# The q projection of two chunks as a Strassen pair, in a transformer layer with sliding attention and a gated FFN on one Trainium2 core

## The chip, the core and the metric

The kernel runs on one core of a Trainium2 chip. The core has a matrix engine (TensorE, PE in the profile), a vector engine (VectorE, DVE), a scalar engine (ScalarE, ACT), GpSimd (POOL) and SyncE (SP). SyncE, ScalarE and GpSimd also issue transfers, each in the order of its own instructions. The metric is the device time of one execution in microseconds. The kernel before was run 8 times: median 770.64 us, from 770.35 to 774.97.

## What is computed

The input x has 2048 rows of 1024 in bf16. First comes attention with 32 heads of 32: each position looks at 8 earlier ones, 2 apart. Then comes a feed-forward network with a product of two projections (F = 3584). Both are added to the input of their part. Cut to what matters:

```python
qkv = layernorm(x) @ wqkv                     # 1024 -> 3 x 1024
logits = sum_d(q[s] * k[s - 2 * w]) * Dh ** -0.5   # w = 0..7, masked where s - 2w < 0
o = sum_w(softmax(logits)[w] * v[s - 2 * w])
h = x + o @ wo
n = layernorm(h)
h2 = h + ((n @ w_gate) * (n @ w_up)) @ w_down
```

## The kernel before, in words

The rows are cut into four chunks of 512 (`TC`). A chunk's normalized rows are kept transposed in `lnT` (feature on the partition). A matmul multiplies a 128x128 block of weights with 128x512 of `lnT`; eight of them make one group for 128 output columns and 512 rows (`mm_group`, L429 to L432, the matmul is on L431). The constant `GROUP_US = 1.73` stands for its time. Its result lies in one of eight banks of psum.

*Projections.* `qkv(c, blocks)` (L434) goes through blocks of 512 columns; q is blocks 0 and 1, k 2 and 3, v 4 and 5. `evac_qkv` (L342) copies each result on ScalarE into a staging tile and stores it on SyncE's queue to `qd`, `kd` or `vd` in memory. `load_qk` and `load_v` (L448, L455) load it back on GpSimd's queue in another layout, with chunk part and head on the partitions, for attention.

*Attention.* `attention(c)` (L468 to L546) is a generator of VectorE work: eight products of q with shifted k (L477), folds over the 32 features (L479 to L487), softmax (Exp on ScalarE), eight products with v (L523) and their sums (L529 to L534). At its end the result `oD` is stored (L536) and loaded back transposed as `oT` in four parts (L539), all on GpSimd's queue, in that order. A chunk's attention starts when the one before has ended (L469).

*Output projection and norm.* `wo_ln2(0)` (L589 to L623) multiplies `oT` by `wo` (L602, 64 matmuls), adds the input on VectorE, and normalizes on VectorE: BATCH_NORM_STATS2 (L183), mean and variance, the row itself, then a transposed load on SyncE's queue. Chunks 1 and 2 use `wo_norm` (L569, matmul L578) and the generator `Norm2.finish` (L562), whose sums and rows are ScalarE's.

*FFN.* `ffn1_first` (L694) computes gate and up of chunk 0 in groups of eight matmuls in 7 blocks of 4; ScalarE copies each result, VectorE multiplies the two (L700). At (b, j) = (4, 2) it calls `wo_1`, which finishes attention 1, runs output projection 1 and starts its norm. `ffn1_second` does chunk 1. For chunks 2 and 3 the FFN already uses Strassen's scheme in Winograd's form (`weight_sums` L796, `activation_sums` L814, `product` L824, `pair_block` L829): of two chunks and two halves of the inner dimension, seven products in place of eight, in fp16 with a power of two as scale. Chunks 0 and 1's down product does the same (`ex`, `ev`, `ey`, `ez`, L944): its sums of weights (`t`, L937) are VectorE's. Class `Scale` (L628 to L656) finds such a power of two: sums of absolute values, one matmul that adds them over the partitions (`total`), a few VectorE operations on one column.

*Order.* No scheduler rearranges anything: each engine runs its instructions in the order in which the program emits them. The order is spread by `Background` (L37 to L75): after each group the main line calls `step(GROUP_US)`, which adds `rate` times that time to a credit, and the generators on its list are advanced until their own estimated times (what they `yield`) have used up the credit. VectorE work of the main line is taken off the credit by `spend`. `finish` runs a generator to its end. So VectorE's order is a mix of attention steps and of the main line's additions, products and norms, fixed when the program is built, and an instruction of VectorE that waits holds all that follows on it.

The main line (L875 to L916) is: q, k of chunk 0 with `load_qk(0)`; chunk 1's q and k; v of chunks 0 and 1; all of chunk 2; q and k of chunk 3; attention 0 is finished; `wo_ln2(0)`; v of chunk 3; the FFN of chunks 0 and 1 with `wo_1` inside; then `wo_adds(2)` (output projection 2, L998), the down products of chunks 0 and 1, `wo_adds(3)`, and the FFN of chunks 2 and 3.

Of the kernel before, what the change touches and what calls it, by code (L numbers as in the profile page):

```python
# [78 lines left out]
def kernel(  # L79
# [46 lines left out]


# [72 lines left out]
    def load_x(c, what, eng):  # L200
        tiles = []
        for t in range(4):
            xt = hp.tile([128, D], BF, tag="h", name=f"{what}{c}_{t}")
            eng.dma_start(xt[:], x[bass.ds(c * TC + t * 128, 128), :])
            tiles.append(xt)
        return tiles
# [52 lines left out]
    class NormOnScalar(Norm1):  # L259
# [16 lines left out]
        def devs(self):  # L276
            nc.scalar.activation(self.nm, self.s, ACTF.Copy, scale=-1.0 / D)
            for t in range(4):
                nc.scalar.activation(self.junk[:], self.xs[t][:], ACTF.Square, bias=self.nm[:, t:t + 1],
                                     accum_out=self.ss[:, t:t + 1])  # L280
                yield "later", self.pace
            nc.scalar.activation(self.rs4[:], self.ss, ACTF.Ln, bias=eps[:], scale=1.0 / D)
# [17 lines left out]
        def rows(self):  # L300
            for t in range(4):
                self.row(t)
                self.transpose(t)
                yield "later", self.pace

# [33 lines left out]

    qkv_in = {}  # L340

    def evac_qkv(c, m, ps):  # L342
        sg = t1k.tile([128, HB + TC], BF, tag="t1k", name=f"sg{c}_{m}")
        nc.scalar.copy(sg[:, HB:HB + TC], ps[:])  # L344
# [5 lines left out]
        if m < 8:  # L350
            nc.sync.dma_start(qd[c][:, 4 * hg:4 * hg + 4, :, :].rearrange("c g d s -> (g d) c s"),
                              sg[:, HB:HB + TC].rearrange("p (c s) -> p c s", c=4))
# [81 lines left out]
    def qkv(c, blocks, last=False):  # L434
        for b in blocks:
            for j in range(4):
                ps = psum.tile([128, TC], F32, tag="mm", name=f"ps{c}_{b}_{j}")
                mm_group(ps, wts["qkv", b], j, lnTs[c])
# [9 lines left out]
    def load_qk(c):  # L448
        qD = att.tile([128, DH, SUB], BF, tag="qD", name=f"qD{c}")
        kD = att.tile([128, DH, SUB + HB], BF, tag="kD", name=f"kD{c}")  # L450
        nc.gpsimd.dma_start(qD[:], qd[c].rearrange("c g d s -> (c g) d s"))
# [16 lines left out]
    def attention(c):  # L468
        while c and c - 1 not in over:  # L469
            yield "later", 1.0  # L470
# [79 lines left out]
    class Norm2(NormOnScalar):  # L550
# [11 lines left out]
        def finish(self):  # L562
            yield from self.devs()
            yield from self.rows()
# [4 lines left out]
    def wo_norm(c):  # L569
# [4 lines left out]
        for t in range(4):  # L574
            for hf in range(2):
# [6 lines left out]
                if hf == 0 and t > 0:  # L582
                    n.sum(t - 1)
                bg.step(GROUP_US)
        n.sum(3)
        retire(2)
        return n

    def wo_ln2(c, at={}):  # L589
        lnT = lnTp.tile([128, KO, TC], BF, tag="lnT", name=f"lnT2_{c}")  # L590
        hs = hss[c]
        mv4, rs4 = ln_tiles(f"2_{c}")

        def norm(t):
            ln = normalize(hs[t], mv4, rs4, t)
            nc.sync.dma_start_transpose(lnT[:, :, bass.ts(t, 128)], ln[:])

        for t in range(4):
            for hf in range(2):
                ps = psum.tile([128, 512], F32, tag="mm", name=f"wo{c}_{hf}_{t}")  # L600
                for kk in range(KO):
                    nc.tensor.matmul(ps[:], lhsT=oTs[c][:, kk, t, :], rhs=wts["wo", c, hf][:, kk, :],  # L602
                                     start=(kk == 0), stop=(kk == KO - 1))
                nc.vector.tensor_tensor(hs[t][:, bass.ts(hf, 512)], ps[:], hs[t][:, bass.ts(hf, 512)], ALU.add)
                if hf == 1:
                    stats(hs[t], mv4, t)
                    rstd_of(mv4, rs4, t, t + 1)
                    bg.spend(1.5)
                elif t > 0:
                    norm(t - 1)  # L610
                    bg.spend(0.55)
                bg.spend(0.7)
                if 2 * t + hf in at:
                    at[2 * t + hf]()
                bg.step(GROUP_US)
        norm(3)
        retire(2)
        for t in range(4):
            rows = hsd[c][:, t, :]
# [734 lines left out]
```

## Time and profile before

| | |
|---|---|
| median of 8 runs | 770.64 us |
| the profiled execution | 770.8 us |
| its span in the trace | 769.0 us |
| TensorE (PE) busy | 763.9 us, 99% |
| weight loads (PEld), beside PE | 350.9 us, 46% |
| VectorE (DVE) busy | 606.2 us, 79% |
| ScalarE (ACT) busy | 513.0 us, 67% |
| GpSimd (POOL) busy | 142.0 us, 18% |
| qkv projections on TensorE after 27.37 us | 136.52 us, 632 matmuls, then 13.81 us, 64 matmuls |
| output projection 0 | 163.89 us, 13.81 us long |
| FFN of chunk 0 starts | 191.51 us |
| output projection 1 starts | 253.67 us |

How to read it: in the page's second part each engine has 40 digits, one for each fortieth of the span (19.2 us), in tenths of busy time; PEclk is TensorE's granted clock in tenths. The chain of waits and the timelines begin a row with the start in us and the length in us, then engine, line and operation, and what is written from what, with a count at the end; a bracket has the idle time of the engine just ahead and what ended it. A row of the groups has a count, then the busy time in us and the mean in ns of one. Back-to-back operations of one engine overlap a little, so that a row's mean can be longer than the step from one to the next.

### The profile page before, as it was taken

What the parts mean: (1) busy time and instruction counts of PE and PEld (TensorE: products, weight loads), DVE (VectorE), ACT (ScalarE), POOL (GpSimd) and SP (SyncE); (2) the same over time, 40 slices, a digit from 0 to 9 for tenths busy, and PEclk for the clock granted to TensorE, in tenths of its full rate; (3) what the DMA queues carried; (4) which work ended last, traced back from release to release, by engine and by line L of the source; (5) the groups of instructions that cost most, each with busy time, mean ns of one, the idle gap of its engine ahead of it and who ended that gap; (6) DMA issues with size and microseconds to landing.
All of it is one profiled execution on the core that took longest, in us unless ns stands there. A gap on an engine that the chain in (4) does not pass through costs nothing.

```text
span 769.0 us, 10302 instructions
## 1 busy us (share of the span) xinstructions
PE 763.9 (99%) x3663; PEld 350.9 (46%) x3663; DVE 606.2 (79%) x718; ACT 513.0 (67%) x979; POOL 142.0 (18%) x152
## 2 busy tenths in 40 slices
PE   8999999999999999999999999999999999999998
PEld 6444444444444444444444444444444444444444
DVE  5629999999999999999998997985454444568863
ACT  4648966423677398777899986836777677788240
POOL 0000000200002000020000001018778677600000
PEclk9999999999999999999999999999999999999999
DMA  8999796999966689579559448673342423730001
GB/s 272 264 258 262 212 268 148 265 312 289 302 221 209 217 297 293 176 243 326 197 184 301 136 159 281 124 198 105 82 110 55 110 74 91 255 128 29 0 29 55
DMA packets 190915, 144.85 MB, mean 188 GB/s; under 512 B 81808, under 2 KB 181136, under 8 KB 188688
## 3 DMA queue, kind: packets, MB, share of 16 engines
q1 hardware_dynamic: 180416, 116.94, 53.9%
q0 software_dynamic: 3584, 22.02, 8.4%
q10 hardware_dynamic: 6864, 5.24, 2.4%
q8 instruction: 28, 0.46, 0.2%
q14 instruction: 23, 0.19, 0.1%
HBM read 110.10 MB, written 27.26 MB: 179 GB/s over the span
## 4 chain that ended last, share of the span: by engine, by line
PE 97%; DVE 2%; DMA 1%; issue 0%; ACTq 0%; DVEq 0%
PE ps L431 21%; PE dx L944 6%; PE py L826 6%; PE pwu L431 6%; PE pwg L431 6%; PE pg L431 6%; PE pz L826 6%; PE px L826 6%; PE pu L431 6%; PE wo L998 4%; PE pv L826 3%; PE ez L944 3%; PE ey L944 3%; PE ex L944 3%; PE dy L944 3%; PE wo L602 2%
## 5 line engine op out<-in xcount | busy, mean ns | idle before, releaser
L431 PE MATMUL ps<-lnT,w_qkv 128*128 128x512 bf16 x736 | 159.6, 379 | 0.0
L431 PEld LDWEIGHTS <-w_qkv 128*128 128x128 bf16 x736 | 71.8, 98 | 86.3 <-issue 0.4
L344 ACT CAST sg<-ps 128x512 bf16<-128x512 f32 x96 | 55.1, 586 | 47.1 <-PE ps L431 44.8
L477 DVE TENSOR_TENSOR prod<-qD,kD 128x4096 bf16<-128x4096 bf16 x32 | 72.2, 2286 | 12.6 <-DMA kD<-kd 12.6
L523 DVE TENSOR_TENSOR pv<-vD,at 128x4096 bf16<-128x4096 bf16 x32 | 72.4, 2286 | 0.2
L826 PEld LDWEIGHTS <-sw 128*128 128x128 f16 x448 | 43.8, 98 | 52.9 <-issue 0.2
L431 PEld LDWEIGHTS <-w_wg 128*128 128x128 bf16 x448 | 43.8, 98 | 52.9
L431 PEld LDWEIGHTS <-w_wu 128*128 128x128 bf16 x448 | 43.8, 98 | 52.9
L826 PE MATMUL px<-lnT,ws 128*128 128x512 bf16 x224 | 55.2, 379 | 0.0
L536 POOL DMA_DIRECT2D od<-oD x4 | 2.2, 544 | 275.8 <-DVE oD L534 275.8
L431 PE MATMUL pwu<-lnT,w_wu 128*128 128x512 bf16 x224 | 52.9, 379 | 0.0
L431 PE MATMUL pwg<-lnT,w_wg 128*128 128x512 bf16 x224 | 52.9, 379 | 0.0
L431 PE MATMUL pg<-lnT,w_wg 128*128 128x512 bf16 x224 | 52.9, 379 | 0.0
L431 PE MATMUL pu<-lnT,w_wu 128*128 128x512 bf16 x224 | 52.9, 379 | 0.0
L826 PEld LDWEIGHTS <-ws 128*128 128x128 f16 x336 | 32.9, 98 | 39.6
L807 POOL TENSOR_TENSOR sw<-ws 128x512 f16<-128x512 f16 x26 | 30.0, 1153 | 82.6 <-PE pv L826 49.1
L944 PEld LDWEIGHTS <-gs 128*128 128x128 f16 (+1 forms) x280 | 27.4, 98 | 33.1
L479 DVE TENSOR_TENSOR prod<-prod 128x4096 bf16<-128x4096 bf16 x16 | 36.6, 2290 | 0.4
L843 ACT COPY py<-px 128x512 f32<-128x512 f32 x28 | 16.0, 570 | 28.5 <-PE px L826 28.5
L808 POOL TENSOR_TENSOR sw<-sw,ws 128x512 f16<-128x512 f16 x26 | 30.0, 1155 | 2.0
L809 POOL TENSOR_TENSOR sw<-ws 128x512 f16<-128x512 f16 x26 | 30.0, 1155 | 0.0
L810 POOL TENSOR_TENSOR sw<-ws,sw 128x512 f16<-128x512 f16 x26 | 30.0, 1155 | 0.0
(334 smaller groups left out, 1474.7 us busy)
## 6 DMA issues: line engine op xcount, KB each, us to landing
w_wg<-in_B_w_gate_dram SPq DMA_DIRECT2D x14, 1024.0 KB, 7.2
w_wu<-in_B_w_up_dram SPq DMA_DIRECT2D x14, 1024.0 KB, 6.6
w_pair<-in_B_w_gate_dram SPq DMA_DIRECT2D x14, 512.0 KB, 4.0
w_pair<-in_B_w_up_dram SPq DMA_DIRECT2D x14, 512.0 KB, 5.3
w_wo<-in_A_wo_dram SPq DMA_DIRECT2D x6, 1024.0 KB, 7.7
w_qkv<-in_A_wqkv_dram SPq DMA_DIRECT2D x5, 1024.0 KB, 11.6
kd<-sg SPq DMA_DIRECT2D x32, 144.0 KB, 4.4
kD<-kd POOLq DMA_DIRECT2D x4, 1152.0 KB, 9.0
```

Of the source, the lines that this page charges most:

```text
L344: nc.scalar.copy(sg[:, HB:HB + TC], ps[:])
L431: nc.tensor.matmul(ps[:], lhsT=wt[:, ko, bass.ts(j, 128)], rhs=rhs[:, ko, :], start=(ko == 0), stop=(ko == KO - 1))
L477: nc.vector.tensor_tensor(prod[:, j], qD[:], kD[:, :, o:o + SUB], ALU.mult)
L479: nc.vector.tensor_tensor(prod[:, :, 0:16], prod[:, :, 0:16], prod[:, :, 16:32], ALU.add)
L523: nc.vector.tensor_tensor(pv[:, j], vD[:, :, o:o + SUB], at[:, w, None, :].to_broadcast((128, DH, SUB)), ALU.mult)
L807: eng.tensor_tensor(sw[:, i, 0], a21, a22, ALU.add)
L808: eng.tensor_tensor(sw[:, i, 1], sw[:, i, 0], a11, ALU.subtract)
L809: eng.tensor_tensor(sw[:, i, 2], a11, a21, ALU.subtract)
L810: eng.tensor_tensor(sw[:, i, 3], a12, sw[:, i, 1], ALU.subtract)
L826: nc.tensor.matmul(ps[:], lhsT=lhs[:, ko, :], rhs=rhs[:, ko, :], start=(fresh and ko == 0), stop=(ko == 3), skip_group_check=not fresh)
L944: nc.tensor.matmul(ps[:, bass.ds(lo, n)], lhsT=lhs[k][:, bass.ts(q, 128)], rhs=rhs[k][:, bass.ds(lo, n)], start=(fresh and k == 0), stop=( ...
L998: nc.tensor.matmul(ps[:], lhsT=oTs[c][:, kk, t, :], rhs=wts["wo", 2, hf][:, kk, :], start=(kk == 0), stop=(kk == KO - 1))
```

## The change

The q projection (blocks 0 and 1) of chunks 2 and 3 is computed together by the same seven-product scheme. The two row halves are the two chunks, the two inner halves are the halves of the 1024 features, and the two output halves are blocks 0 and 1. For each of four positions m the program makes seven products of four matmuls. `q_pair(0)` does two of the four before output projection 0, `q_pair(2)` the others behind it, with two groups of chunk 3's v in between.

What this needs: a power of two as scale for q's weights (four sums of absolute values, two on VectorE, two on ScalarE, and one small matmul); the conversion of both weight blocks to fp16 in place (VectorE); 16 sums of weights (VectorE); sums of the two chunks' `lnT` (`q_row_sums`, 12 operations, and `q_last_sum`, one, VectorE). Of the 16 results eight are evacuated by ScalarE and eight by VectorE, which adds the product `p5` from a staging tile. Chunk 1's q uses the converted weights too.

Around it: the order of the projections is other; attention 1 does not start before `q_last_sum`; the load of chunk 3's x waits for the landing of chunk 0's k, and the load of chunk 0's q for the transposes of chunk 1 (one-element copies on GpSimd that touch both). Output projection 0 uses `wo_norm` with `devs=False`: sums and squares on ScalarE, the four rows on VectorE in place of BATCH_NORM_STATS2; the rate of `Background` is 1.06 after it (1.03 before). The steps of `abs_down` are closer together, and a scale's total in `wo_adds(2)` comes two groups later. The diff, cut to its core:

```diff
-    def load_x(c, what, eng):
+    def load_x(c, what, eng, after=None):
         tiles = []
         for t in range(4):
             xt = hp.tile([128, D], BF, tag="h", name=f"{what}{c}_{t}")
+            if after is not None and t == 0:
+                nc.gpsimd.tensor_copy(xt[:, 0:1], after)
...
+        def row_on_vector(self, t):
+            ln = lnp.tile([128, D], BF, tag="ln", name=f"ln{self.what}{self.c}_{t}")
+            nc.vector.tensor_scalar(ln[:], self.xs[t][:], self.rs4[:, t:t + 1], self.nb[:, t:t + 1], ALU.mult, ALU.add)
+            bg.spend(0.52)
+            self.lns[t] = ln
...
+    scale_q = Scale("q", 4)
...
-        nc.scalar.copy(sg[:, HB:HB + TC], ps[:])
+        if c == 1 and m < 8:
+            nc.scalar.activation(sg[:, HB:HB + TC], ps[:], ACTF.Copy, scale=scale_q.inv)
+        else:
+            nc.scalar.copy(sg[:, HB:HB + TC], ps[:])
...
-    def load_qk(c):
+    def load_qk(c, after=None):
         qD = att.tile([128, DH, SUB], BF, tag="qD", name=f"qD{c}")
         kD = att.tile([128, DH, SUB + HB], BF, tag="kD", name=f"kD{c}")
+        if after is not None:
+            nc.gpsimd.tensor_copy(qD[:, 0, 0:1], after)
...
-        while c and c - 1 not in over:
+        while c and (c - 1 not in over or c == 1 and "t3" not in qsum):
...
+        def sum_dev(self, t):
+            col = slice(t, t + 1)
+            self.sum(t)
+            nc.scalar.activation(self.nm[:, col], self.s[:, col], ACTF.Copy, scale=-1.0 / D)
+            nc.scalar.activation(self.junk[:], self.xs[t][:], ACTF.Square, bias=self.nm[:, col],
+                                 accum_out=self.ss[:, col])
+
+        def finish(self, devs=True):
+            if devs:
+                yield from self.devs()
+            else:
+                self.sum_dev(3)
+                yield "later", self.pace
+                self.rstds()
+                yield "later", self.pace
+            yield from self.rows(self.row if devs else self.row_on_vector)
...
+                if hf == 1 and t > 0 and not devs:
+                    n.sum_dev(t - 1)
...
-    def wo_ln2(c, at={}):
-        lnT = lnTp.tile([128, KO, TC], BF, tag="lnT", name=f"lnT2_{c}")
-        hs = hss[c]
-        mv4, rs4 = ln_tiles(f"2_{c}")
...
-                if hf == 1:
-                    stats(hs[t], mv4, t)
-                    rstd_of(mv4, rs4, t, t + 1)
-                    bg.spend(1.5)
-                elif t > 0:
-                    norm(t - 1)
-                    bg.spend(0.55)
...
+            yield "later", 2.0 * GROUP_US
             if p + 2 < 7:
                 load(p + 2)
-            yield "later", 4.9 * GROUP_US
+            yield "later", 1.9 * GROUP_US
...
-    qkv(0, range(1, 4))
-    load_qk(0)
...
+    def q_abs(k):
+        src = wts["qkv", k // 2][:, bass.ts(k % 2, 4), :]
+        if k < 2:
+            nc.vector.tensor_reduce(scale_q.l1[:, k:k + 1], src, mybir.AxisListType.XY, ALU.add,
+                                    apply_absolute_value=True)
+        else:
+            scale_q.add(k, src, att.tile([128, 4, 512], BF, tag="oT", name=f"junk_q{k}")[:])
...
+    def q_convert():
+        for r in range(2):
+            wt = wts["qkv", r]
+            nc.vector.tensor_scalar(f16(wt[:]), wt[:], scale_q.s, None, ALU.mult)
+        bg.spend(2.6)
+        bg.add(q_weight_sums(), bg.now)
+
+    def q_weight_sums():
+        for m in range(4):
+            a11, a12, a21, a22 = (q_weight(r, kh, m) for r in range(2) for kh in range(2))
+            if m < 2:
+                rooms = [f16(hp.tile([128, D], BF, tag="h", name=f"qs{m}_{i}")[:]) for i in range(2)]
+                s1, s2, s3, s4 = (r[:, bass.ts(i, 512)].rearrange("p (k c) -> p k c", k=4) for r in rooms
+                                  for i in range(2))
+            else:
+                s1, s2, s3, s4 = (t1k.tile([128, 4, 128], F16, tag="t1k", name=f"qs{m}_{i}")[:] for i in range(4))
+            nc.vector.tensor_tensor(s1, a21, a22, ALU.add)
+            nc.vector.tensor_tensor(s2, s1, a11, ALU.subtract)
+            nc.vector.tensor_tensor(s3, a11, a21, ALU.subtract)
+            nc.vector.tensor_tensor(s4, a12, s2, ALU.subtract)
+            qsum[m] = (s1, s2, s3, s4)
+            yield 1.7
...
+    def q_row_sums():
+        while 0 not in over:
+            yield "later", 0.5
+        lo, hi = slice(0, 4), slice(4, 8)
+        b11, b21, b12, b22 = (lnTs[c][:, ks, :] for c in (2, 3) for ks in (lo, hi))
+        t1, t2, t4 = ([t1k.tile([128, TC], F16, tag="t1k", name=f"qt{i}_{k}")[:] for k in range(4)] for i in (1, 2, 4))
+        for k in range(4):
+            nc.vector.tensor_tensor(t1[k], b12[:, k, :], b11[:, k, :], ALU.subtract)
+            nc.vector.tensor_tensor(t2[k], b22[:, k, :], t1[k], ALU.subtract)
+            if k % 2:
+                yield 1.7
+        for k in range(4):
+            nc.vector.tensor_tensor(t4[k], b21[:, k, :], t2[k], ALU.subtract)
...
+    def q_last_sum(room):
+        t3 = room[:, 2:4, :].rearrange("p a c -> p (a c)").bitcast(F16).rearrange("p (k c) -> p k c", k=4)
+        nc.vector.tensor_tensor(t3, lnTs[3][:, 4:8, :], lnTs[3][:, 0:4, :], ALU.subtract)
+        qsum["t3"] = [t3[:, k, :] for k in range(4)]
...
+    def q_product(ps, lhs, rhs, fresh):
+        for ko in range(4):
+            nc.tensor.matmul(ps[:], lhsT=lhs[:, ko, :], rhs=rhs[ko], start=(fresh and ko == 0), stop=(ko == 3),
+                             skip_group_check=not fresh)
+        bg.step(GROUP_US / 2)
...
+        xb, yb, zb, ub, p5 = [[None] * 2 for _ in range(5)]
+        sw = [qsum[m0 + i] for i in two]
+        a11, a12, a21, a22 = ([q_weight(r, kh, m0 + i) for i in two] for r in range(2) for kh in range(2))
+        for i in two:
+            xb[i] = bank("x", i)
+            q_product(xb[i], a11[i], b11, True)
+            yb[i] = bank("y", i)
+            nc.scalar.copy(yb[i][:], xb[i][:])
+        for i in two:
+            v = bank("v", i)
+            q_product(v, sw[i][0], t1, True)
+            p5[i] = room[:, i, :]
+            nc.scalar.activation(p5[i], v[:], ACTF.Copy, scale=inv)
+        t3 = qsum["t3"]
+        for i in two:
+            q_product(yb[i], sw[i][1], t2, False)
+            zb[i] = bank("z", i)
+            nc.scalar.copy(zb[i][:], yb[i][:])
+        for f in between[0:1]:
+            f()
+        for i in two:
+            q_product(xb[i], a12[i], b21, False)
+            out_scalar(2, m0 + i, xb[i])
+            q_product(zb[i], sw[i][2], t3, False)
+            ub[i] = bank("u", i)
+            nc.scalar.copy(ub[i][:], zb[i][:])
+            out_vector(3, 4 + m0 + i, zb[i], p5[i])
+        for f in between[1:2]:
+            f()
+        for i in two:
+            q_product(yb[i], sw[i][3], b22, False)
+            out_vector(3, m0 + i, yb[i], p5[i])
+            q_product(ub[i], a22[i], t4, False)
+            out_scalar(2, 4 + m0 + i, ub[i])
+
+    qkv(0, [1, 2], at={(1, 1): lambda: q_abs(0), (1, 2): lambda: q_abs(2), (1, 3): lambda: q_abs(1),
+                       (2, 0): lambda: q_abs(3), (2, 2): scale_q.rows})
+    qkv(0, [3], at={(3, 2): scale_q.total, (3, 3): q_convert})
+    load_qk(0, after=lnTs[1][:, 0, TC - 1:TC])
+    start_attention(0)
+    qkv(1, [2])
     bg.finish(rows2)
+    xtiles[3] = load_x(3, "x", nc.sync, after=qkv_in["k", 0][:, 0, 0:1])
+    pump(6)
+    state["live"] += 1
     for t in range(4):
         norm1[2].transpose(t)
-    xtiles[3] = load_x(3, "x", nc.sync)
-    pump(6)
-    state["live"] += 1
-    bg.add(norm1[3].sums(), bg.now + 18.0)
-    start_attention(0)
+    bg.add(norm1[3].both(), bg.now + 14.0, first=True)
     sums = abs_down()
-    bg.add(sums, bg.now + 25.0, first=True)
-    qkv(1, range(4))
+    bg.add(sums, bg.now + 36.0, first=True)
+    qkv(1, [3, 0, 1])
     qkv(0, range(4, 6))
     load_v(0)
-    bg.add(norm1[3].rows(), bg.now, first=True)
     qkv(1, range(4, 6))
     start_attention(1)
     pump(pair_at)
-    qkv(2, range(6))
+    qkv(2, range(2, 6))
+    rows_q = q_row_sums()
+    bg.add(rows_q, bg.now, first=True)
+    qkv(3, [2, 3], last=True)
+    hss[0] = load_x(0, "h", nc.sync)
+    state["live"] += 1
+    qkv(3, [4], last=True)
+    bg.finish(atts[0])
+    bg.finish(rows_q)
+    room_q = wpool.tile([128, 4, TC], F32, tag="w", name="room_q")
+    q_last_sum(room_q)
+    bg.spend(bg.credit)
+    bg.rate = 1.06
+    q_pair(0, room_q)
+    bg.spend(1.0)
+    norm2 = [wo_norm(0, devs=False)]
+    norm2.append(norm2[0].finish(devs=False))
+    bg.add(norm2[1], bg.now, first=True)
+    qkv(3, [5], js=(0, 1))
+    q_pair(2, room_q, between=(lambda: qkv(3, [5], js=(2,)), lambda: qkv(3, [5], last=True, js=(3,))))
+    bg.finish(norm2[1])
+    retire(3)
+    lnT2_0 = norm2[0].lnT
...
-    hT0 = ffn1_first(nxt[0], {(4, 2): wo_1})
+    hT0 = ffn1_first(lnT2_0, {(4, 2): wo_1})
...
-                4: in_turn(total_h1, lambda: pull(1)), 6: lambda: pull(1)})
+                4: lambda: pull(1), 6: in_turn(total_h1, lambda: pull(1))})
```

## The prediction, made before the changed kernel was run

> **What bounds the kernel now.** I read the page's engine rows first, then the chain of waits, then VectorE's and GpSimd's timelines around the hand-overs that the change touches.
>
> ```profile
> PE 763.9 (99%) x3663; PEld 350.9 (46%) x3663; DVE 606.2 (79%) x718; ACT 513.0 (67%) x979; POOL 142.0 (18%) x152
> ...
> DVE  5629999999999999999998997985454444568863
> ...
> PEclk9999999999999999999999999999999999999999
> ```
>
> TensorE is busy all the time at full clock; its own waits add up to 2.1 us, all before 12 us. But from about 57 to 480 us VectorE is full as well (nines), and a share of 79% hides that. The chain shows TensorE's work in order:
>
> ```profile
> 27.37 136.52 PE ps L431 x632
> 163.89 13.81 PE wo L602 x64
> 177.70 13.81 PE ps L431 x64
> 191.51 1.73 PE pg L431 x8
> ...
> 253.67 13.81 PE wo L578 x64
> ...
> 449.33 24.17 PE ey L944 x112
> ```
>
> No gaps: 136.52 us for 632 matmuls, 0.216 us each, 1.727 for a group of 8. Anything that makes TensorE wait is added to the end; anything taken from TensorE is a gain only while VectorE's results still come in time. VectorE's timeline:
>
> ```profile
> 52.50 4.49 DVE L477 TENSOR_TENSOR prod<-qD,kD 128x4096 bf16<-128x4096 bf16 x2 [12.56 <-DMA kD<-kd]
> ...
> 235.11 2.29 DVE L534 TENSOR_TENSOR oD<-oD,pv 128x4096 bf16<-128x4096 bf16 x1
> ...
> 419.13 0.18 DVE L639 TENSOR_REDUCE rowd<-l1d 128x1 f32<-128x23 f32 x1 [0.42 <-ACT junkb L635]
> ...
> 422.18 0.16 DVE L647 COPY totd<-ey 128x1 f32<-128x1 f32 x1 [1.46 <-PE ey L645]
> ```
>
> Attention 0 starts at 52.50 after 12.56 us of waiting for a transfer. From then on its only idle of note is 0.42 and 1.46 us near 420. Attention 1 ends at 235.11 + 2.29 = 237.40. From there a chain of transfers on GpSimd's queue leads to output projection 1:
>
> ```profile
> 237.69 0.54 POOL L536 DMA_DIRECT2D od<-oD  x1 [63.54 <-DVE oD L534]
> 244.71 3.54 POOL L539 DMA_DIRECT2D oT<-od  x4 [6.47 <-DMA od<-oD]
> ```
>
> The store lands after 6.3 us, the first of the four loads of oT lands 3.7 us after 244.71, at 248.4: 11.0 us after VectorE's last sum. TensorE wants it at 253.67. The cover is 5.2 us.
>
> **The change, part by part.** *TensorE.* 128 matmuls of chunks 2 and 3's q become 7 x 16 = 112: 16 x 0.216 = 3.45 us less, and one small matmul for the scale more (0.05 to 0.2). Without stalls output projection 0 starts 12 groups earlier less the 7 that the first pair of blocks takes: 155.3, the FFN at 188.1 (191.51 before), output projection 1 at 250.3 (253.67).
>
> *VectorE before attention 0.* Two sums of absolute values over 128x2048 are new. Nearest row: the 1224 ns of L484 (128x1024 to fp32), so 2.4 us each. The Trainium skill ("VectorE: DVE Perf Modes", "The perf-mode tier table") has a reduction at one element per cycle only, which comes to an estimated 2.1; either fits VectorE's idles of 2.85 and 2.12 us before 25.3. Two conversions as in L802 (1279 ns), 16 weight sums of 0.4: 9.0 us, in the 12.56 us of idle. So VectorE is free by 51, and attention 0 ends at 136.8 as before (136.73). Without that cover it would be late by 9. Two more absolute sums on ScalarE (1.93 each) delay the transposes of chunk 1 on its queue by 3 us; the competing qD load is now gated behind these: 0 to 1 us.
>
> *Around output projection 0.* These rows price what comes:
>
> ```profile
> L523 DVE TENSOR_TENSOR pv<-vD,at 128x4096 bf16<-128x4096 bf16 x32 | 72.4, 2286 | 0.2
> ...
> L863 DVE SCALAR_TENSOR_TENSOR up<-py,ibgu,p 128x512 bf16<-128x512 f32 x14 | 10.5, 751 | 13.7 <-PE py L826 13.7
> ```
>
> Row sums of the inputs: 12 x 0.39 = 4.7, the last sum 1.14. They are ready at 139.6, 140.1 and 142.7; the products that use them begin at 144.9, 146.7 and 149.3. TensorE does not wait, with 5 us to spare. oT of chunk 0 lands at 136.8 + 11.7 (its own trip in this trace) = 148.5, and is wanted at 155.3.
>
> But attention 1 is queued behind all this. Ledger for VectorE from the end of attention 0 to the end of attention 1 (100.7 us before): row sums +5.8; eight evacuations as L863, 0.75 less 0.08 of overlap, +5.4; waits for TensorE at the first two adds of output projection 0 +2.4 (VectorE arrives at 155.8, the groups end at 157.1 and 158.8, and attention steps are queued behind); two more g·u products that now come first in VectorE's order, +0.7; eight BATCH_NORM_STATS2 (676 ns) and their small operations fall away, -6.6. Sum +7.7; operation by operation in the changed kernel's order, which the program fixes, +8.0. **Attention 1 ends at 245.4**, and because of the waits in it this hardly depends on when attention 0 ends.
>
> *Output projection 1.* 245.4 + 11.0 = 256.4. The other two trips of this trace took 11.7 and 12.6; the shortest and longest store and load give 8.2 and 13.9, so 253.6 to 259.3. I take 11.0, as the same queue carries the same neighbours. TensorE comes at 250.3 and waits 6.1 us: the 3.4 won are gone, and it is 2.7 late.
>
> Here a rule of the skill speaks against taking only the row. "TensorE: Matmul & The Clock Gate", "What's actually happening", says that an idle window of about 3.4 us halves the clock until about 3.4 us of work have passed: 1.7 us more. The PEclk row has nines only, but TensorE never idles that long in it. By the row +2.7 here, by the rule +4.4. I take the row for the forecast, since the next step covers both.
>
> *The first FFN's start.* The norm's last row on VectorE ends at 186.6; its transposed load is issued at 187.0 behind the q stores on SP's queue and takes 3.1 to 3.3 (such loads before): 190.3 against 188.1, a hold of 2.2 us. It falls inside the wait for oT 1 and costs nothing by itself; without that wait it costs 2.2.
>
> *Where VectorE's delay goes.* TensorE is 2.7 late, VectorE 8.0. VectorE has hardly any idle in which to make it up: 7.2 are left at the first add of output projection 2 (402.85 before). The two waits at 419 and 422 give 1.9 back: 5.3. Its weight differences for the down product end at 450.4 before (446.55 + 3.96, less overlap). The second one is wanted 7 matmuls (1.51 us) into the product at 449.33, at 450.8: a slack of 0.4. After: 455.8, so this product starts no earlier than 454.3, **5.0 late**, whatever is lost up to 4.9 before it. Then VectorE has idle again (fours and fives), and nothing later ties.
>
> *Early holds.* The load of chunk 3's x is now gated on a landing, and the fifth block of weights queues behind it on SP's queue: landing at 66.9 to 69 against a need at 67.1. With the transposes I take 0.5 us (0 to 3). It delays the waits of VectorE for TensorE with it, so it is added.
>
> Sum against the profiled execution: span 769.0 + 5.0 + 0.5 = 774.5, and 1.8 around it (770.8 - 769.0) = 776.3. This execution is 0.16 above the median of 770.64: **776.1**. The moves of the scale's total and of the absolute sums, and the rate of the interleaving, I count at nothing beyond the order already used; they hide behind VectorE's delay, and cost up to 0.7 if it were gone.
>
> **Rivals.** *The saving stays (faster).* One mechanism: VectorE's order holds, but oT of chunk 1 is there when TensorE comes, at 250.3. Then attention 1 must end by 239.3, 6.1 us earlier than in my sum. For it: only the sizes of new operations are unknown, and a faster norm would do part. Against: evacuations and row sums have near rows. 770.64 - 3.2 = 767.4. It decides there: for each us later than 239.3 TensorE loses one, and at 243 the gain is gone. Chance 0.14.
> *Half of it comes back.* A trip of 8.2 us, and VectorE regains 3 us in waits that vanish; the down product starts 1 us late or so: 771.5. For it: the bounds of the trip. Against: VectorE's nines. Chance 0.12.
> *Early holds and a half clock.* Holds of 2 to 3 before projection 0, which push VectorE as well, or the slow clock after the long wait on top: 776.1 + 3 = 779. Chance 0.15.
> *The forecast*: 0.59, with its own range of 774 to 778.
>
> **How the numbers follow.** A measurement of this kernel tells about 0.3% (2.3 us) from no change: below 768.3 is faster, above 772.95 slower. So faster 0.14, same 0.12, slower 0.74. The range from 770.0 to 779.5 leaves out the first rival and the upper end of the third, under 0.2.
>
> **What would show it.** Attention 1's last sum ends near 245.4; TensorE stands idle about 6 us before output projection 1, released by the load of oT; VectorE's waits at 419 and 422 are gone; the second down product starts near 454, released by VectorE. No wait of TensorE in the q products. I am wrong if attention 1 ends before 240, if TensorE waits in the Strassen products themselves, or if VectorE has caught up at 420.

## The result and the profile after

The changed kernel took 779.0 us (median of 11 runs, 774.35 to 781.39) against 770.64: ratio 1.0094, 95% interval 1.0078 to 1.0111. It is slower, and within the range of 770.0 to 779.5, but 2.9 us above the forecast of 776.1. The profiled execution took 774.09 us, with a span of 772.3, 3.3 more than before. So there are two questions: where the 3.3 us of this execution come from, and why the others scatter up to 7 us above it. Before scatters much less (770.1 to 772.0 in nearly all of its 31 runs).

First the engine rows of the page after:

```profile
PE 762.5 (99%) x3648; PEld 349.9 (45%) x3648; DVE 623.5 (81%) x754; ACT 531.3 (69%) x1009; POOL 144.7 (19%) x154
...
PE   9999999999999799999999999999999999999998
...
DVE  6779989999999799999999998985553444578863
...
PEclk9999999999999999999999999999999999999999
```

15 matmuls fewer, as forecast, and VectorE has 17 us more. New is the one 7 in TensorE's row, in the slice from 251 to 270 us, and in the same slice of VectorE's. TensorE's waits after (engine, line, what for: us in all, times, longest):

```profile
PE wo L653 <- DMA oT<-od: 3.9, 1, 3.9
...
PE qy L949 <- ACT qy L981: 0.8, 1, 0.8
...
PE pg L488 <- DMA qd<-sg: 0.4, 1, 0.4
```

The big one is output projection 1, waiting for oT of chunk 1, as forecast. The chain of waits there:

```profile
240.17 2.30 DVE oD L596
...
242.75 5.10 DMA od<-oD
...
248.56 6.57 DMA oT<-od
...
255.18 15.67 PE wo L653 x64
```

Attention 1 ends at 242.45 by VectorE's timeline (237.40 before), oT lands at 255.13 (248.4 before), and TensorE had been done at 251.29. The load took 6.6 us in place of 3.7, since a burst of other loads is under way. In the table by stretches (the columns are the stretch, its length, busy us and instructions of PE, PEld, DVE, ACT and POOL, then the granted clock, the DMA engines' share and GB/s) before has, while oT is loaded:

```profile
244.70:248.40 3.70, 3.70 (x19) 1.70 (x18) 3.65 (x5) 2.20 (x4) 3.69 (x5) 1.00 0.46 113
248.40:252.00 3.60, 3.60 (x18) 1.60 (x17) 3.56 (x5) 3.21 (x9) 0.40 (x1) 1.00 1.06 298
```

and the kernel after, in the stretch of its own load:

```profile
248.60:252.00 3.40, 2.69 (x13) 1.00 (x11) 3.37 (x4) 1.90 (x6) 3.40 (x4) 1.00 1.07 353
```

Before, the first part is through when the burst begins at 248.4; after, it lies in it. The two have moved towards each other: the FFN's next weights, a part of that burst (`w_wu` and `w_wg`, 1 MB each), are requested 2.4 us earlier (244.41 and 246.93, before 246.80 and 249.32), as TensorE is ahead, and oT 3.9 us later. That the late start alone does not do it, the run with the old norm shows below.

The projection itself is slower too. TensorE's timeline has it before and after:

```profile
253.51 13.98 PE L578 MATMUL wo<-w_wo,oT 128*128 128x512 bf16 x64
```

```profile
255.18 15.67 PE L653 MATMUL wo<-w_wo,oT 128*128 128x512 bf16 x64 [3.89 <-DMA oT<-od]
```

(The chain has 13.81 for the first of these, since it leaves out the overlap with the matmul ahead; after an idle time there is none.) The table by stretches shows why it takes longer:

```profile
255.00:259.00 4.00, 3.82 (x11) 1.49 (x12) 1.67 (x2) 0.00 (x0) 0.00 (x0) 0.60 1.03 268
259.00:263.00 4.00, 4.00 (x20) 1.75 (x18) 2.47 (x2) 1.15 (x2) 0.00 (x0) 0.97 0.38 157
```

The granted clock is 0.60 in the 4 us from the end of the wait: 11 matmuls in 3.82 us where 18 fit. The page's PEclk row does not show it, since a slice of 19 us is an average that still reads 9. So TensorE is 255.18 - 253.51 = 1.7 us late at the projection's start and takes 15.67 - 13.98 = 1.7 us longer for it. That makes 3.4 at its end, which is the whole 3.3 of the execution.

And the second down product, which I had as the step that sets the end? VectorE around it:

```profile
424.06 0.18 DVE L372 TENSOR_REDUCE rowd<-l1d 128x1 f32<-128x23 f32 x1 [0.43 <-ACT junkb L368]
...
425.56 0.15 DVE L380 COPY totd<-ey 128x1 f32<-128x1 f32 x1
...
449.93 3.96 DVE L1085 TENSOR_TENSOR t<-b,w_dn 128x3584 f16<-128x3584 f16 x2
```

The wait for ScalarE at 424 is still there, only the 1.46 at the copy is gone. The differences end at 453.89, and are wanted 1.51 us into the product, which the chain has here:

```profile
452.58 24.18 PE ey L1092 x112
```

That is 454.09: 0.2 us to spare. VectorE is 3.4 late there and TensorE 3.3 (449.33 before). VectorE adds nothing, but it would not let TensorE be much earlier either.

### The profile page after: what moved, and what is told of

It reads as the page before. It is cut to its first block, busy times and chain, and to the rows that moved or that the text cites. A ratio compares the mean times of both kernels' runs of the same rounds, so it can differ in the third digit from the quotient of the medians.

```text
span 772.3 us, 10333 instructions
## 1 busy us (share of the span) xinstructions
PE 762.5 (99%) x3648; PEld 349.9 (45%) x3648; DVE 623.5 (81%) x754; ACT 531.3 (69%) x1009; POOL 144.7 (19%) x154
## 4 chain that ended last, share of the span: by engine, by line
PE 86%; DVE 10%; DMA 2%; issue 1%; ACT 0%; SPq 0%; DVEq 0%; POOLq 0%
PE ps L488 16%; PE dx L1092 6%; PE py L837 6%; PE pz L837 6%; PE pwu L488 6%; PE pwg L488 6%; PE px L837 6%; PE wo L1146 4%; PE pv L837 3%; PE ez L1092 3%; PE ey L1092 3%; PE ex L1092 3%; PE pg L488 3%; PE pu L488 3%; PE dy L1092 3%; PE wo L653 2%
## 5 line engine op out<-in xcount | busy, mean ns | idle before, releaser
L488 PE MATMUL ps<-lnT,w_qkv 128*128 128x512 bf16 x608 | 132.2, 379 | 0.0
L488 PEld LDWEIGHTS <-w_qkv 128*128 128x128 bf16 (+1 forms) x608 | 59.3, 98 | 70.9
L402 ACT CAST sg<-ps 128x512 bf16<-128x512 f32 x72 | 41.6, 586 | 19.6 <-PE ps L488 10.0
L818 POOL TENSOR_TENSOR sw<-ws 128x512 f16<-128x512 f16 x26 | 30.0, 1153 | 82.3 <-PE pv L837 49.0
L653 PE MATMUL wo<-w_wo,oT 128*128 128x512 bf16 x128 | 29.7, 395 | 3.9 <-DMA oT<-od 3.9
```

The source lines that it names most:

```text
L488: nc.tensor.matmul(ps[:], lhsT=wt[:, ko, bass.ts(j, 128)], rhs=rhs[:, ko, :], start=(ko == 0), stop=(ko == KO - 1))
L818: eng.tensor_tensor(sw[:, i, 0], a21, a22, ALU.add)
```

## Experiments

Theory A: the loss is the wait for oT of chunk 1 and the low clock after it, since VectorE's new work (the evacuations above all) delays attention 1. Rivals: B, VectorE's delay sets the time at the second down product, and the wait only comes first; C, the amount of new work does not matter but its order; D, the scatter has a cause of its own. Each run is given with its median, its range and its ratio to the kernel before on the same chip.

**The control.** The changed kernel once more.

> The changed kernel once more, as the control beside the next three. Its executions lay between 774.4 and 781.4 us, and the mean granted clock goes with it: 0.998 at 774 to 775, 0.991 to 0.993 at 779 to 781. If the wait for oT of chunk 1 is the only place where TensorE stands still long enough, a slow execution shows a longer wait there or more slow matmuls after it. If there is a second place, its trace shows low clock in another slice.

Median 779.5 us (774.67 to 782.47), ratio 1.011 (1.0081 to 1.0139). The trace has the same wait, 4.3 us. The granted clock of each run goes with its time: 0.998 at 774.7 and 775.9, 0.995 at 777.7, 0.991 in the three above 781. In time, 0.002 x 773 = 1.5 us of TensorE are lost in the quickest and 0.009 x 780 = 7.0 in the slowest. That is 5.5 of the 7.8 us between them. The trace is of the quickest, so where the others lose the rest is not seen.

**No idle time before output projection 1.** One edit, in `wo_1`:

```diff
         bg.finish(atts[1])
+        keep = psum.tile([128, TC], F32, tag="mm", name="keep")
+        for i in range(18):
+            nc.tensor.matmul(keep[:], lhsT=ones[:], rhs=lnT2_0[:, 0, :], start=True, stop=True)
         n = wo_norm(1)
```

> 18 matmuls that nobody reads (3.9 us) are put ahead of output projection 1, where TensorE would stand idle. If the slow clock comes from that idle time: the projection takes 13.8 us in place of 15.7, the time is 1.9 us lower at 772.4 to 772.6, the clock is 1.0 in every execution and the executions above 777 are gone. If the slow executions have another cause: the spread up to 781 stays.

Median 775.1 us (773.17 to 776.64), ratio 1.0058 (1.0046 to 1.007); clock 1.0 in every run, none above 777. TensorE's timeline:

```profile
251.50 4.05 PE L1062 MATMUL keep<-lnT,ones 128*128 128x512 bf16 x18
255.97 13.99 PE L653 MATMUL wo<-w_wo,oT 128*128 128x512 bf16 x64 [0.42 <-DMA oT<-od]
```

The projection starts as late as in the control (255.97 against 255.99) and takes 13.99 us in place of 15.48. So the low clock follows from the idle time, and matmuls that nobody reads win 1.5 us in the profiled execution and 4.4 in the median. D is out for the executions above 777: they need this idle time. The 3.5 us of scatter that are left, all at full clock, are not explained.

**A like idle time without the Strassen pair.** The kernel before, with one edit:

```diff
-    hT0 = ffn1_first(nxt[0], {(4, 2): wo_1})
+    hT0 = ffn1_first(nxt[0], {(3, 3): wo_1})
```

> The kernel before, with output projection 1 three steps earlier, at (3, 3): nothing of the Strassen pair is in it. TensorE comes at 243.3, oT lands near 248.4, and it stands idle about 5 us. If an idle time of 4 to 5 us brings the slow clock and the spread by itself: 770.6 + 5 + 1.9 = 777.5 at the fastest, granted clock 0.998 or less, and other executions some us higher. If the spread belongs to the changed kernel's other parts: 775 to 776, clock 1.0, no spread.

Median 779.1 us (778.76 to 779.97), ratio 1.0116 (1.01 to 1.0131), clock 0.996 to 0.998. TensorE's timeline, and the stretch after the wait:

```profile
248.45 16.35 PE L578 MATMUL wo<-w_wo,oT 128*128 128x512 bf16 x64 [5.52 <-DMA oT<-od]
```

```profile
249.00:253.00 4.00, 4.00 (x11) 1.36 (x10) 0.92 (x2) 0.00 (x0) 0.00 (x0) 0.50 1.03 294
```

5.5 us of idle time, then half the clock and 2.4 us more for 64 matmuls: the low clock comes without the changed part. But the scatter of the four executions is small (1.2 us), and none falls to 0.991. So one idle time of 5.5 us alone does not make the slowest executions.

**VectorE's evacuations.** ScalarE evacuates the eight results that VectorE did, and the addition of p5 in them is left out:

```diff
-            nc.vector.scalar_tensor_tensor(sg[:, HB:HB + TC], ps[:], inv, p5, ALU.mult, ALU.add)
-            bg.spend(0.75)
+            nc.scalar.activation(sg[:, HB:HB + TC], ps[:], ACTF.Copy, scale=inv)
```

> The eight evacuations of the Strassen pair that VectorE makes are made by ScalarE, and the addition of p5 in them is left out. VectorE has 5.4 us less to do between 150 and 193. If VectorE's added work delays attention 1: its last sum ends about 5 us earlier than 242.5, oT lands near 250, TensorE waits less than 0.5 us, and the time is 768.5 to 770. If it is the hold of attention 1 and the order, not the amount of work: attention 1 ends after 241 and the time stays above 773.

Median 769.2 us (768.99 to 769.94, 20 runs), ratio 0.9981 (0.9975 to 0.9988). VectorE's timeline has attention 1's last sum:

```profile
234.14 2.28 DVE L596 TENSOR_TENSOR oD<-oD,pv 128x4096 bf16<-128x4096 bf16 x1
```

It ends at 236.42, 6.0 us earlier for 5.4 of work taken away. oT's first part lands in 3.7 us again, there is no wait for it, the clock is 1.0, the scatter is gone. C is out for the evacuations: their amount counts. Of the 3.45 us of matmuls saved only 1.5 of span remain; the waits of TensorE that are left:

```profile
PE ey L378 <- DVE rowbd L373: 1.0, 1, 1.0
PE qy L949 <- ACT qy L980: 0.5, 1, 0.5
...
PE ey L1091 <- DVE t L1084: 0.3, 1, 0.3
```

1.8 us, of which 1.3 are VectorE's at the down product: B's place, at a small size.

**The row sums.** The 12 sums are left out; plain halves stand in the products:

```diff
-            nc.vector.tensor_tensor(t1[k], b12[:, k, :], b11[:, k, :], ALU.subtract)
-            nc.vector.tensor_tensor(t2[k], b22[:, k, :], t1[k], ALU.subtract)
...
-            nc.vector.tensor_tensor(t4[k], b21[:, k, :], t2[k], ALU.subtract)
...
-        qsum["b"] = (cells(b11), cells(b21), t1, t2, t4, cells(b22))
+        qsum["b"] = (cells(b11), cells(b21), cells(b12), cells(b22), cells(b21), cells(b22))
```

> The 12 row sums on VectorE (4.7 us between 136.7 and 141.5) are left out; the products take plain halves of the inputs in their place. The order of everything else is the same. Theory A (VectorE waits for TensorE at the first adds of output projection 0 anyway, 1.6 us in the changed kernel): the 4.7 us turn into more waiting there, attention 1 ends at 242 to 242.6, TensorE waits about 4 us for oT and the time stays at 774 to 782 with the same spread. Theory B (all work added to VectorE counts): attention 1 ends near 238 and the time is 769 to 770.

Median 774.8 us (773.98 to 775.5), ratio 1.0055 (1.0042 to 1.0068). Attention 1 ends at 242.53 in place of 242.45, and TensorE waits 4.5 us for oT. 4.7 us of work cost nothing, as expected, but not for the reason that I gave. The four executions also lack the scatter that I expected, with the same idle time. VectorE's timeline:

```profile
141.94 1.23 DVE L938 TENSOR_TENSOR room_q<-lnT 128x2048 f16<-128x2048 bf16 x1 [4.14 <-ACT w_ring L368]
...
158.32 0.69 DVE L655 TENSOR_TENSOR h<-wo,h 128x512 bf16<-128x512 f32 x1 [0.98 <-PE wo L653]
```

The last sum goes to a tile of the weight ring that is free only when ScalarE has finished with `w_ring`, at 141.9. VectorE waits 4.14 us for that. In the changed kernel the row sums lie in this time, with 0.36 us of waiting left. The wait at the adds of output projection 0 is behind that and has not grown (0.98 us in both). Here the run stands for "work ahead of a wait is free", and not for the wait that I named.

**The norm.** `wo_ln2(0)` of the kernel before, with the interleaving that it books, in place of `wo_norm(0, devs=False)`:

```diff
-    norm2 = [wo_norm(0, devs=False)]
-    norm2.append(norm2[0].finish(devs=False))
-    bg.add(norm2[1], bg.now, first=True)
+    nxt = wo_ln2(0)
...
-    bg.finish(norm2[1])
     retire(3)
-    lnT2_0 = norm2[0].lnT
+    lnT2_0 = nxt[0]
```

> Chunk 0's second norm goes back to VectorE as before (BATCH_NORM_STATS2, rows within output projection 0), all else as in the changed kernel. VectorE has about 4.5 us more in front of the rest of attention 1. Theory A: attention 1 ends 4 to 5 us later, near 247, TensorE waits 8 to 9 us for oT, and the time is 778.5 or more at the fastest. Rival: the norm on ScalarE and SyncE was itself a cause of delay (the hold ahead of the first FFN), and the time is as now or lower.

Median 793.1 us (791.61 to 794.68), ratio 1.0293 (1.0279 to 1.0306). TensorE's waits:

```profile
PE wo L653 <- DMA oT<-od: 10.3, 1, 10.3
PE wo L1177 <- DMA oT<-od: 5.4, 1, 5.4
```

Attention 1 ends at 251.17, 8.7 us later and not 4 to 5. A later attention is late too: the second row is output projection 3, at 493.90. The hold ahead of the FFN (0.4 us) is gone, which is next to nothing. So without the norm's move, and the interleaving that goes with it, the Strassen pair would cost 14 us more.

This run also tells what lengthens the load of oT. It starts 7.7 us later than in the changed kernel, and its first part lands in 3.8 us:

```profile
256.30:260.10 3.80, 0.00 (x0) 0.00 (x0) 0.00 (x0) 0.00 (x0) 3.80 (x5) 0.50 0.44 128
```

The DMA engines' share is 0.44, as before the change (0.46), and not 1.07.

**Output projection 1 later.** Two steps later, and one:

```diff
-    hT0 = ffn1_first(lnT2_0, {(4, 2): wo_1})
+    hT0 = ffn1_first(lnT2_0, {(5, 0): wo_1})
```

> Output projection 1 is put two steps of the first FFN later, at (5, 0) in place of (4, 2): TensorE comes 6.9 us later and oT is there. Theory A (the loss is the wait for oT and the slow clock after it): the wait of 3.9 us and the 1.9 us of slow matmuls go, 774.3 - 5.8 = 768.5, and the executions no longer spread. Theory B (VectorE's delay sets the time, and the wait for oT only came first): the weight differences of the down product still end near 453, TensorE waits up to 5 us before the second down product, released by VectorE, and the time stays at 772 to 775.

Median 776.3 us (774.59 to 781.57), ratio 1.0089 (1.0065 to 1.0114). The wait for oT is gone, and its like has come back later:

```profile
PE pwg L488 <- DMA lnT<-ln: 4.6, 1, 4.6
PE qy L949 <- ACT qy L981: 1.7, 1, 1.7
```

Chunk 1's norm hangs on the projection, and the second half of the FFN starts with its result. Neither theory had this wait. It comes with the low clock and with executions of 780 and 781.6, so the scatter is not tied to output projection 1. But not every idle time of that length brings it: the runs without the row sums (4.5 us) and of the kernel before (5.5 us) have none, in four executions each.

```diff
-    hT0 = ffn1_first(lnT2_0, {(4, 2): wo_1})
+    hT0 = ffn1_first(lnT2_0, {(4, 3): wo_1})
```

> Output projection 1 one step later, at (4, 3): TensorE comes 3.5 us later, at 254.8, when oT lands at 255.2 to 256. The norm of chunk 1 also ends 3.5 us later; two steps later it made TensorE wait 4.6 us ahead of the second FFN half, so here about 1. Theory A: 774.3 - 5.8 + 0.5 + 1 = 770.0, 769.5 to 771.5, and few slow executions. Theory B (VectorE's weight differences are the next bound): TensorE waits 3 us or more ahead of the second down product, 772.5 or more.

Median 771.9 us of 14 runs, ratio 1.0025 (1.001 to 1.004). Eight lie between 770.02 and 772.02, all with clock 1.0; six between 774.0 and 776.16, with 0.996 to 0.998. The profiled execution has a span of 768.6:

```profile
PE wo L653 <- DMA oT<-od: 1.1, 1, 1.1
...
PE ey L1092 <- DVE t L1085: 0.2, 1, 0.2
```

The wait is 1.1 us, and with it no low clock. TensorE is now 0.2 us early for VectorE's differences at the down product. Theory A gave 770.0, and this is the lower group; B's 3 us are not there. Six of 14 at 774 or more are not the few that I expected; the trace is of the lower group, so what they wait for is not seen.

**Cheaper evacuations.** GpSimd adds p5 after ScalarE has evacuated:

```diff
-            nc.vector.scalar_tensor_tensor(sg[:, HB:HB + TC], ps[:], inv, p5, ALU.mult, ALU.add)
-            bg.spend(0.75)
+            nc.scalar.activation(sg[:, HB:HB + TC], ps[:], ACTF.Copy, scale=inv)
+            nc.gpsimd.tensor_tensor(sg[:, HB:HB + TC], sg[:, HB:HB + TC], p5, ALU.add)
```

> The eight evacuations of VectorE are made by ScalarE, and GpSimd adds p5 in place, so that nothing is left out. Theory A (only the amount of VectorE's work after projection 0 matters): as the run without p5, 769.0 to 769.8, no wait of TensorE for oT, clock 1.0. Rival: GpSimd's additions hold up VectorE beside them or the transfers behind them on its queue, and a part of the wait for oT is back: 770.5 or more.

Median 774.4 us (774.15 to 775.12), ratio 1.0053 (1.004 to 1.0066), clock 1.0. The rival holds: GpSimd's additions hold up VectorE. VectorE beside them, and a later one of them:

```profile
151.43 2.07 DVE L546 TENSOR_TENSOR t<-prod 128x1024 f32<-128x1024 bf16 x1
153.53 1.53 DVE L548 TENSOR_TENSOR t<-t 128x512 f32<-128x512 f32 x1
155.10 1.27 DVE L549 TENSOR_TENSOR lg<-t 128x256 f32<-128x256 f32 x1
```

```profile
159.29 2.50 POOL L971 TENSOR_TENSOR sg<-sg,room_q 128x512 bf16<-128x512 bf16 x1 [3.21 <-ACT sg L970]
```

The three took 1.22, 0.68 and 0.43 in the changed kernel: 0.85 us more on each. Four more between 184 and 195 lose 0.84 to 0.96 us each; the seven come to 6.0. Attention 1 ends at 241.53, so only 0.9 of the 6.0 us are won. For oT TensorE stands idle only 0.7 us (oT lands at 253.02, and the projection starts at 253.05). The rest of the loss is spread; the two longest waits are these (`issue` is a wait for nothing that the profile shows):

```profile
PE l1psh L378 <- ACT junkb L368: 1.7, 1, 1.7
PE pg L488 <- issue: 1.5, 1, 1.5
```

Next, VectorE adds p5 itself, but from bf16 tiles after ScalarE's evacuation (0.34 us each). Two versions have a rate of 1.25 up to output projection 1 as well, at (4, 3) and at (4, 2); a third has the old rate, at (4, 3):

```diff
-            nc.vector.scalar_tensor_tensor(sg[:, HB:HB + TC], ps[:], inv, p5, ALU.mult, ALU.add)
-            bg.spend(0.75)
+            nc.scalar.activation(sg[:, HB:HB + TC], ps[:], ACTF.Copy, scale=inv)
+            nc.vector.tensor_tensor(sg[:, HB:HB + TC], sg[:, HB:HB + TC], p5, ALU.add)
+            bg.spend(0.4)
...
+    bg.rate = 1.25
```

> A version meant to be faster than both, nothing left out. ScalarE evacuates VectorE's eight results, VectorE only adds p5 from a bf16 tile (0.34 us each in place of 0.67: 2.6 us less), the first FFN's interleaving rate is 1.25 until output projection 1 (three products of gate and up less ahead of attention 1's end, 1.0 us), and output projection 1 is at (4, 3). Theory A: attention 1 ends at 238 to 239, oT lands by 252, TensorE comes at 254.8 and does not wait, clock 1.0 in all executions, 768.9 to 769.8. Theory B (VectorE's weight differences come next): a wait ahead of the second down product of over 1.5 us, 770.5 or more.

> The same with output projection 1 at (4, 2) as in the changed kernel: TensorE comes at 251.3, oT lands at 250.5 to 252. Theory A: a wait of 0 to 0.7 us, too short for the slow clock, 769 to 770, nearly no slow executions. If the slow executions have a cause of their own in the changed order and not the idle time: some lie above 774 here and in the version at (4, 3) too.

Medians 787.9 and 785.4 us, ratios 1.022 (1.02 to 1.0241) and 1.0201 (1.0186 to 1.0216): both expectations were wrong by 15 us or more. Attention 1 does end at 239.15 and 239.42, and TensorE does not wait for oT. But it waits right behind output projection 1. The version at (4, 3), TensorE's waits and VectorE's first addition of that projection:

```profile
PE l1psh L378 <- DVE rowbh L373: 4.6, 1, 4.6
PE pg L488 <- DVE h L655: 4.3, 1, 4.3
PE pwg L488 <- DMA lnT<-ln: 2.2, 1, 2.2
```

```profile
271.16 0.68 DVE L655 TENSOR_TENSOR h<-wo,h 128x512 bf16<-128x512 f32 x1
```

The projection began at 253.65, so its first group was ready at 255.4, and VectorE comes for it 16 us later: the higher rate has put nearly three rounds of attention 2 ahead of it in VectorE's order (one round and two products in the earlier version at (4, 3)), and the projection's eight results hold all eight banks. The rate decides whose delay it is, and makes none of VectorE's work go away.

> As the version at (4, 3) with ScalarE's evacuations and VectorE's short additions of p5, but with the interleaving rate left at 1.06, so that no more of attention 2 stands ahead of output projection 1's additions in VectorE's order than the real saving allows; nothing left out. Theory A (the raised rate alone made the last two versions slow: it put attention 2 ahead of these additions): attention 1 ends near 240, oT lands near 252.5, TensorE comes at 254.8 and does not wait, VectorE reaches the first addition at about 256.6 as the first group ends, no wait of the FFN behind it; 768.8 to 769.8 and no slow executions. Theory B (ScalarE's additional evacuations are what made them slow): waits of TensorE for VectorE or ScalarE of 5 us or more remain, 774 or more.

Median 774.9 us (772.22 to 776.45), ratio 1.0047 (1.003 to 1.0064). 13 us better than with the higher rate, so that was the larger part, but not theory A's 769. Attention 1 ends at 242.93, no earlier than in the changed kernel, where 240 was expected. ScalarE's fourth evacuation and VectorE's addition behind it:

```profile
160.07 0.69 ACT L970 ACTIVATE sg<-qy,ibq 128x512 bf16<-128x512 f32 x1 [6.06 <-DMA vd<-sg]
```

```profile
160.79 0.43 DVE L971 TENSOR_TENSOR sg<-sg,room_q 128x512 bf16<-128x512 bf16 x1 [3.66 <-ACT sg L970]
```

The evacuation waits for its staging tile, which an earlier store of v still reads, and VectorE waits for the evacuation: the work that VectorE is spared turns into waiting. In the run without p5 this evacuation waited 0.80 us. In the changed kernel the wait (4.8 us) lies one evacuation later, where VectorE does not depend on it. TensorE's waits, and the table by stretches after each of them:

```profile
PE l1psh L378 <- ACT junkb L368: 2.5, 1, 2.5
PE qy L949 <- ACT qy L982: 2.1, 1, 2.1
```

```profile
180.00:184.00 4.00, 4.00 (x14) 1.54 (x13) 3.98 (x5) 1.26 (x3) 0.00 (x0) 0.71 0.66 124
...
413.00:417.00 4.00, 3.39 (x10) 1.29 (x11) 3.97 (x7) 4.00 (x9) 0.00 (x0) 0.68 1.07 357
```

Both waits are for ScalarE, and both bring the low clock. But ScalarE is not short of time: from 140 to 190 us it is busy for 34.7 us here and for 36.7 in the run without p5, where TensorE waits only 0.5 us at the same product. After the late evacuation it starts the norm's first sum at 162.45 and not at 159.33, and the copy that TensorE waits for comes behind that norm. Ahead of the second wait ScalarE stood 4.61 and 1.50 us for VectorE, which is as late as in the changed kernel. So theory B's cause, too many evacuations on ScalarE, is not what the trace shows. The stores of v were issued 2.5 us later here than without p5 (146.43 and 143.96); why is open. No version with all of the work in it was faster than before; the one at (4, 3) comes within 0.25% of it.

## Why the prediction was right or wrong

*The direction and the place: right.* TensorE's saving is there (TensorE reached the first Strassen product at 142.65, with none of the early holds, and lost 1.3 us from there to the FFN; 0.8 of that in the q products, where I had said that it would not wait). It is lost at output projection 1, because VectorE's new work delays attention 1. Taking away the evacuations brings the time to 769.2, undoing the norm's move brings it to 793.

*Attention 1 ends at 245.4: too late by 2.9.* Measured 242.45, +5.1 in place of +8.0. Output projection 0 starts 0.6 earlier than forecast (154.74, and not 155.3), so that VectorE's waits at its first two adds come to 1.6 and not 2.4. In the terms of the ledger: the evacuations were worth 6.0 and not 5.4, the 12 row sums nothing and not 4.7, the norm's move 8.7 (with its interleaving) and not 6.6. The row sums were free because of a wait that the ledger lacks: the last sum's room is held by ScalarE until 141.9. These terms do not add up to the 2.9; the rest is open.

*The trip of 11.0 us: too short.* 12.7, within the bounds of 8.2 to 13.9. "The same queue carries the same neighbours" was the wrong reason: the neighbours are a burst of loads with a place in time, and trip and burst had moved into each other. With attention 1 2.9 earlier, the trip 1.7 longer and TensorE there at 251.29 and not at 250.3, the wait was 3.9 and not 6.1.

*The clock: the step that failed.* "By the row +2.7 here, by the rule +4.4. I take the row." The row had no idle time of that length and could say nothing, and I let it speak. The rule of the Trainium skill ("TensorE: Matmul & The Clock Gate", "What's actually happening") gave an estimate of 1.7 us, and the trace has 1.7; the other runs with an idle time of 4.3 us or more ahead of this projection have 1.4 to 2.5. The traces differ from it in the length of the idle time, about 3.4 us in the rule: with ScalarE's evacuations and the old rate 2.1 and 2.5 us were enough, while 1.7 us (projection 1 at (5, 0)) and 2.2 us (higher rate, (4, 3)) brought nothing.

*The second down product 5.0 late: wrong as the step that sets the end.* VectorE is 3.4 late there, not 5.3, and TensorE just as late: 0.2 us of slack. Without TensorE's delay it shows, with 0.2 to 1.3 us. The forecast of 776.1 stood 2.0 above the profiled execution with a step that did not bind and without the one that did: 5.0 from the down product in place of 3.4 from the wait and the clock. That it came so close is in part luck.

*The median: not foreseen.* 2.9 us above the forecast and above its own range of 774 to 778, since six of the 11 executions lose 5 to 7 us of granted clock, and the profiled one 1.5. The wide range holds the median by 0.5 us only. Nearest to it is the third rival (779), with the slow clock after the long wait; the early holds that it also names did not come. That the executions above 777 need idle time of TensorE is shown (18 unread matmuls end them). How it grows to 7 us is open: no trace of such an execution was taken, and one idle time of 5.5 us in the kernel before did not bring it. A guess is that lost clock makes a later wait long enough to lose it again.

*VectorE before attention 0: right.* The two absolute sums took 2.23 and 2.28 us (2.1 to 2.4 forecast), the weight sums ended at 48.6, and attention 0 ended at 136.75 (136.8 forecast). *The FFN's hold* was 0.4 and not 2.2. *The rate of 1.06 and the moved totals*, counted at nothing, were not tested by themselves.

## What to carry to other kernels

Work taken from the engine that bounds the kernel is a gain only if the engine that feeds it has room for what replaces it; a share of 79% says nothing about a stretch of 400 us in which it has none. Count a long idle time on TensorE as more than its length (in these traces every one of 3.9 us or more ahead of dense matmuls, and some of 2.1 to 2.5), and look for the lost clock in stretches of a few us, since a slice of the page hides it. When a transfer moves in time, look at what else is under way at the new place. An engine that is spared work gains nothing if it then waits for what the work had hidden. And moving a step out of one wait asks what hangs on that step next.

## What was not expected of the hardware

An idle time that was only 4 us long cost 1.5 to 1.7 us of clock in the profiled executions of the changed kernel, and its executions lost up to 7 us in a way that is open. Matmuls that nobody reads cost less than the idle time that they fill. GpSimd's additions on 128x512 and VectorE's operations beside them slowed each other: 0.84 to 0.96 us more on each of VectorE's seven, which take 0.43 to 2.29 us alone, and 1.2 to 3.2 us for one of GpSimd's (its sums of weights of that shape take 1.15 in the kernel before).
